# Warm-up products on one tile, another order of loads, and a written plan of the feed-forward groups in an attention and feed-forward kernel

## The chip, the core and the metric

The kernel runs on one core of a Trainium2 chip. The metric is device time in microseconds (us); the kernel before has a median of 373.9 us over 11 runs (372.59 to 376.28).

## What is computed

Sixty-four heads (8 batches of 8 heads, 576 positions, head size 64) of causal attention with a bias that falls with the running sum of relu(s), and then a feed-forward layer with a hard-swish gate over all 4608 tokens:

```python
scores = q @ k.T / 8                       # per head, 576 x 576
cum    = cumsum(maximum(s, 0))
scores = where(causal, -1e9, scores + minimum(-(cum_i - cum_j), 0))
x      = softmax(scores) @ v               # -> [4608, 512], heads side by side
h      = x @ w_in                          # [512, 2048]
g      = h * clip(h + 3, 0, 6) / 6
out    = g @ w_out                         # [2048, 512]
```

q, k, v, s, the weights and the output are float32; products take float16 operands and accumulate in float32.

## The kernel before

**Pairs and stages.** Heads are taken in 32 pairs, four to a batch (`PPB = 4`). One turn of the loop `for p in range(NP)` (L677) is a stage: scores of both heads of pair p, the exponentials, the products with v, normalisation, and the transposes that bring x into the layout of the feed-forward part. The scores of a head come in three pieces of 512 columns (`scores`, L277) and a corner for both heads (`corner`, L328). ScalarE takes the exponential (L322), VectorE applies the mask from p=5 on (L324). For p <= 4 the mask is a product instead (L285), so that the wide stair rows are not needed. `av` (L362) multiplies with v, `norm` (L390) divides by the row sum (L395, L396).

**How a pair comes in.** `load_qk` (L103) and `load_v` (L122) bring float32 into three raw buffers each (`NRAW = 3`), on the queue of SP. GpSimd casts them to float16 (`cast_qk` L173, `cast_v` L180). Pairs 0 to 3 are transposed on TensorE (L220) and copied by `order` (L199, on line L206). Pairs 4 to 8 come through a casting transfer that GpSimd issues (L110), are transposed at L228 and copied at L238. From pair 9 on the transfer engines transpose (`crossbar_qk`, L251), and `spread` copies into place. Four rows of each pair's q and k tile hold the bias; `load_aug` (L135) copies them from `rows_of`, which is worked out at the start from s (`cum1` to `cum6`, L602 to L630). Pair 0 takes its bias by products with `rows_of` and `picked` instead (L269, L314). `set_stair` (L560) fills further rows of a buffer for the pairs from 5 on.

**The front.** After the first loads are issued, `warm(22)` (L578) puts 22 idle products on TensorE (L574), each into a new tile W of one buffer with the tag "o". Then come the two transposes of pair 0 (L654, L655), `warm(4)`, and the loop.

**Feed-forward groups.** The layer works on 9 blocks of 512 tokens. `m1` (L448) is one group of four products x @ w_in (L439) into one of two "ph" banks, then ScalarE's relu with bias 3 into `tr` (L454) and VectorE's min and multiply into `gT` (L455), which frees the bank. `m2` (L459) is a group of four products gT @ w_out (L466); every fourth of a token tile is followed by a copy (L475) and a store (L477). A stage has fixed places where `group()` (L502) is called: seven at p=4 and eight from p=5 on. `group` takes m1 and m2 in turn: m1 if the last was not m1 and the block's x is there, else m2 if `m2_ready` allows it (two more m1 done than it needs, and from block 1 on 12 more m1 than m2, `LAG = 12`), else the place stays empty. Block n can begin when batch n of attention is done (block 8 with batch 7). After the last stage the rest is done without attention between.

**Queues.** Each engine works its instructions in the order in which the code issues them. SP's queue holds loads, the transposing transfers and the stores; GpSimd's holds the casts, the casting transfers (tok, w_in, w_out) and the bias rows. A transfer that waits for a buffer holds all behind it on its queue. The parts of w_in and w_out are placed by the table `weights_in` (L669) and line L664: w_in part 0 ahead of the loop, part 1 at p=2, part 2 at p=3, part 3 and the first two of w_out at p=4, and two of w_out at each of p=5, 6, 7.

Of the kernel before, what the change touches and what calls it, by code (L numbers as in the profile page):

```python
# [9 lines left out]
F32 = mybir.dt.float32  # L10
# [8 lines left out]
def kernel(  # L19
# [10 lines left out]
    nc = tc.nc  # L30
# [7 lines left out]
    NP = NHEADS // 2  # L38
    PPB = H // 2
# [4 lines left out]
    NPE = 2 * PPB + 1  # L44
# [1 line left out]
    NRAW = 3  # L46
    VW = 66
    NROW = 1
    NWARM = (22, 4)

# [49 lines left out]
    def flat(p):  # L100
        return p < PPB or p >= NPE

    def load_qk(p, i, eng=nc.sync):  # L103
        b, h0 = p // PPB, 2 * (p % PPB)
        src = (q, k)[i][b, h0 : h0 + 2]
        if not flat(p):
            if not i:
                tok = work.tile([128, 24 * D], F16, tag="tok", bufs=4, name="tok")
                toks[p] = tok[0:96].rearrange("p (i h e d) -> p i h e d", i=2, h=2, e=6)
            nc.gpsimd.dma_start(  # L110
                out=toks[p][:, i].rearrange("p h e d -> p h (e d)"),
                in_=src.rearrange("h (p e) d -> p h (e d)", e=6),
            )
# [345 lines left out]
    def m2(n, i):  # L459
        t4, fq = 2 * (i // 8) + i % 2, i % 8 // 2  # L460
        if fq == 0:
            po = psum.tile([128, 512], F32, tag="po", bufs=2, name="po")
            pos[n, t4] = po
        po = pos[n, t4]
        for ft in range(4 * fq, 4 * fq + 4):
            mm(  # L466
                po,
                lhsT=gTs[n][:, ft, t4 * 128 : (t4 + 1) * 128],
                rhs=w_out_sb[:, ft, :],
                start=(ft == 0),  # L470
                stop=(ft == NFT - 1),
            )
        if fq == 3:
            ob = work.tile([128, 512], F32, tag="ob", bufs=3, name="ob")
            nc.vector.tensor_scalar_mul(out=ob, in0=po, scalar1=1.0 / 6.0)  # L475
            r = n * 512 + t4 * 128
            nc.sync.dma_start(out=out[r : r + 128, :], in_=ob)  # L477
# [2 lines left out]
    m2_list = [(n, i) for n in range(NBLK) for i in range(16)]  # L480
    done = {1: 0, 2: 0}
    last = [2]
    tail = [False]
    LAG = 12

    def m1_ready():
        i = done[1]
        if i >= len(m1_list):
            return False
        return (512 * m1_list[i][0] + 511) // SEQ < x_done[0] // PPB  # L490

    def m2_ready():
        i = done[2]
        if i >= len(m2_list):
            return False
        n, j = m2_list[i]
        need = 16 * n + (4 * (j // 2) + 4 if j < 8 else 16)
        if done[1] == len(m1_list):
            return True
        return done[1] >= max(need + 2, i + LAG if n else 0)  # L500

    def group():  # L502
        a, c = m1_ready(), m2_ready()
        if not (a or c):
            return False
        if a and (last[0] == 2 or (tail[0] and not c)):
            m1(*m1_list[done[1]])
            done[1] += 1
            last[0] = 1
        else:  # L510
            if c:
                m2(*m2_list[done[2]])
                done[2] += 1
            last[0] = 2
        return True


    C = {}
# [8 lines left out]
    load_qk(0, 0)  # L527
    load_qk(0, 1, nc.scalar)
    nc.scalar.preload_act_table_set("natural_log_exp_and_others")
    for p in (1, 2):  # L530
        for i in range(2):
            load_qk(p, i)
        load_v(p - 1, nc.sync)
    for i in range(NROW):
        fill(nc.gpsimd, qks[i][64:68, :, :, :], 0.0)
    fill(nc.gpsimd, ident, 0.0)
# [32 lines left out]
    fill(nc.vector, xT[:, 0, 0:512], 0.0)  # L569

    def warm(n):
        for _ in range(n):
            W = psum.tile([128, 512], F32, tag="o", name="W")
            nc.tensor.matmul(  # L574
                W, lhsT=xT[:, 0, 0:128], rhs=xT[:, 0, 0:512], start=True, stop=True
            )
# [65 lines left out]
    cum1(0, V)  # L642
    cum2(0)
    cast_qk(0, nc.scalar.copy)
    for i in range(2):
        load_qk(3, i)
    load_v(2, nc.sync)
    cum3(0, V)
    nc.scalar.copy(out=rows_of[0][0:32, 0, 0:SEQ], in_=C["c"][0:32])
    cum4(0, V)  # L650
# [5 lines left out]
    warm(NWARM[1])  # L656
    for g in range(1, 2 * NROW):
        pick(g)
    load_aug(1, nc.gpsimd)
    cast_qk(1)  # L660
    load_aug(2, nc.gpsimd)
    cast_v(0)
    cast_qk(2)
    load_w_in(0)  # L664
    cast_v(1)


    I, U = load_w_in, load_w_out
    weights_in = {  # L669
        2: ((I, 1),),  # L670
        3: ((I, 2),),
        4: ((I, 3), (U, 0), (U, 1)),
        5: ((U, 2), (U, 3)),
# [2 lines left out]
    }  # L676
    for p in range(NP):  # L677
        nxt = p + 1 < NP
        if p + 3 < NP:
            load_v(p + 3, nc.sync)  # L680
        if p == 1:
            nc.sync.dma_start(out=stair_sb, in_=stair_dram.ap())
        if NPE <= p + 4 < NP:
            for i in range(2):
                load_qk(p + 4, i)
        if PPB <= p < PPB + 3:
            set_stair((p + 1) % NQK, nc.gpsimd.tensor_copy)
            load_aug(p + 1, nc.gpsimd)
        c = p + 2
        if p and c < NP and flat(c):  # L690
            cast_qk(c)
            if c >= NPE:
                crossbar_qk(c)
        if p and nxt:
            cast_v(p + 1)
        if p and p < NP - 2 and not PPB <= p + 1 < PPB + 3:
            load_aug(p + 2, nc.gpsimd)
        for fn, c in weights_in.get(p, ()):
            fn(c)
        if p and PPB <= p + 3 < NPE:  # L700
            for i in range(2):
                load_qk(p + 3, i)
        if p == 10:
            load_s(1, (nc.sync,) * 4)
            fill(nc.gpsimd, rows_of[1][:, 0, :], 1.0)
        if p == 11:
            cum1(1, nc.gpsimd)
        if p == 12:
            cum2(1)
            nc.gpsimd.tensor_copy(out=rows_of[1][0:32, 0, 0:SEQ], in_=C["c"][0:32])  # L710
        if p == 13:
            cum3(1, nc.gpsimd)
            cum4(1, nc.gpsimd)
        if p == 13:
            cum5(1, nc.gpsimd)
            cum6(1, nc.gpsimd)

        def get(i):
            if p + 1 < NPE:
                transpose(p + 1, i)  # L720
            elif nxt:
                spread(p + 1, i)

        if p < PPB:
            scores(p, 0, 0)
            scores(p, 0, 1)
# [12 lines left out]
            av(p, 0, 0)  # L739
            scores(p, 1, 2)  # L740
            av(p, 0, 1)
            norm(p, 0)
            continue

        if p == PPB:
            early[0] = False
            scores(p, 0, 0)
            av(p - 1, 1, 0)
            m1_begin(0, 0, NKC - 1)
            av(p - 1, 1, 1)  # L750
            norm(p - 1, 1)
            scores(p, 0, 1)
            m1_begin(0, 1, NKC - 1)
            transpose_x(p - 1)
            group()
            group()
            scores(p, 0, 2)
            get(0)
            nc.vector.tensor_scalar(
                out=masks, in0=shut, scalar1=65504.0, scalar2=None, op0=ALU.add  # L760
            )
        else:
# [24 lines left out]
        av(p, 0, 1)  # L787
        norm(p, 0)
        group()
# [6 lines left out]
    group()  # L796
    group()
    transpose_x(p)
    tail[0] = True
    while group():  # L800
        pass
# [28 lines left out]
```

## Time and profile before

| | |
|---|---|
| median of 11 runs | 373.9 us |
| profiled execution, own time | 375.43 us |
| its span | 373.4 us |
| TensorE products busy (PE) | 358.1 us, 96% |
| VectorE (DVE) | 244.2 us, 65% |
| ScalarE (ACT) | 219.7 us, 59% |
| GpSimd (POOL) | 130.6 us, 35% |
| m2 products L466 | 576, 146.1 us |
| m1 products L439 | 576, 149.0 us |
| idle products L574 | 26, 585 ns each |
| HBM read, written | 37.36 MB, 9.44 MB |

All times come from one profiled execution. A line of a timeline has start, duration, engine, source line, operation, what is written from what, the tile's size, how often; in square brackets the idle time just before and what ended it. PE is TensorE's products, PEld its loads of weights, SPq or POOLq the issue of a transfer. In the rows over the span each digit is a fortieth of it, in tenths.

### The profile page before, as it was taken

To read this page: it belongs to the slowest core of one execution; us is meant where nothing else is said; L and a number is where in the kernel's file an instruction comes from. 1 tells how busy PE (TensorE), PEld (TensorE's weight loads), DVE (VectorE), ACT (ScalarE), POOL (GpSimd) and SP (SyncE) were. 2 spreads that over 40 slices of the span, in tenths; PEclk is the share of its full clock that TensorE was granted. 3 is DMA by queue.
4 is the path that set the end of the run, shared out by engine and by line. 5 is a ranking of instruction groups with operands and counts; after the bars stand their busy time and mean duration, and the time that the engine had idled before them with its cause. 6 is when DMAs were issued, how large, how long until landed. Compare 5 with 4: busy or idle time off the path is not lost.

```text
span 373.4 us, 7780 instructions
## 1 busy us (share of the span) xinstructions
PE 358.1 (96%) x2892; PEld 193.3 (52%) x2892; DVE 244.2 (65%) x551; ACT 219.7 (59%) x382; POOL 130.6 (35%) x227
## 2 busy tenths in 40 slices
PE   7999888989999999999999999999999999999995
PEld 1277555555555555555555555555555544444442
DVE  7148687757689987676767676767675635445541
ACT  3158776766667666666666666666666443434420
POOL 4849896553255933333333333333100000000000
PEclk9999999989999999999999999999999999999999
DMA  9989999994889698969787999697711101101102
GB/s 184 205 164 163 207 206 217 185 197 108 177 208 169 155 202 159 206 148 197 163 185 170 204 149 208 143 190 164 125 62 37 56 0 58 56 0 59 56 36 77
DMA packets 158262, 52.76 MB, mean 141 GB/s; under 512 B 146969, under 2 KB 153113, under 8 KB 158225
## 3 DMA queue, kind: packets, MB, share of 16 engines
q1 hardware_dynamic: 148608, 45.58, 58.9%
q0 software_dynamic: 8352, 6.25, 10.6%
q10 hardware_dynamic: 1264, 0.44, 0.6%
q8 instruction: 22, 0.36, 0.4%
q14 instruction: 16, 0.12, 0.1%
HBM read 37.36 MB, written 9.44 MB: 125 GB/s over the span
## 4 chain that ended last, share of the span: by engine, by line
PE 88%; DVE 8%; ACT 2%; issue 1%
PE po L466 32%; PE ph L439 31%; PE O L373 7%; PE S L303 7%; PE W L574 4%; PE S L292 3%; DVE gT L455 2%; DVE qk L238 2%; ACT tr L454 1%; PE pt L220 1%; DVE x L396 1%; PE ptx L410 1%; DVE qk L206 1%; DVE P L324 1%; PE S L285 1%
## 5 line engine op out<-in xcount | busy, mean ns | idle before, releaser
L455 DVE SCALAR_TENSOR_TENSOR gT<-tr,ph 128x512 f16<-128x512 f32 x144 | 98.5, 684 | 86.8 <-ACT tr L454 85.7
L439 PE MATMUL ph<-xT,w_in_sb 128*128 128x512 f16 x576 | 149.0, 380 | 1.5 <-DVE gT L455 0.9
L466 PE MATMUL po<-w_out_sb,gT 128*128 128x512 f16 x576 | 146.1, 379 | 1.2 <-DVE x L396 1.2
L454 ACT ACTIVATE tr<-ph,bias 128x512 f32<-128x512 f32 x144 | 99.0, 687 | 80.4 <-PE ph L439 71.0
L322 ACT ACTIVATE P<-S 128x512 f16<-128x512 f32 x192 | 111.8, 594 | 45.7 <-PE S L292 24.5
L439 PEld LDWEIGHTS <-w_in_sb 128*128 128x128 f16 x576 | 51.8, 98 | 45.2 <-issue 1.7
L466 PEld LDWEIGHTS <-gT 128*128 128x128 f16 x576 | 49.8, 97 | 46.8 <-DVE x L396 1.4
L138 POOL DMA_DIRECT2D qk<-rows_of x62 | 36.0, 582 | 73.5 <-PE S L303 62.4
L303 PE MATMUL S<-qk 68*128 68x448 f16 (+3 forms) x256 | 49.8, 276 | 0.8 <-ACT P L322 0.8
L373 PE MATMUL O<-va,P 128*128 128x65 f16 x896 | 48.2, 193 | 0.8 <-DVE x L396 0.8
L373 PEld LDWEIGHTS <-P 128*128 128x128 f16 x896 | 39.8, 97 | 15.0 <-DVE x L396 1.3
L182 POOL CAST va<-vraw 128x512 f16<-128x512 f32 x32 | 19.8, 617 | 53.3 <-issue 29.9
L303 PEld LDWEIGHTS <-qk 68*128 68x128 f16 x256 | 24.0, 99 | 25.7 <-issue 1.7
L206 DVE COPY qk<-jt 64x768 f16<-64x768 f16 x92 | 33.5, 365 | 3.5 <-DMA jt<-tok 2.1
L178 POOL CAST tok<-raw 128x576 f16<-128x576 f32 x52 | 34.2, 686 | 1.9 <-DMA raw<-in_k_dram 1.3
L396 DVE TENSOR_TENSOR x<-O,rl 128x320 f16<-128x320 f32 x64 | 31.5, 492 | 2.2
L475 DVE TENSOR_SCALAR ob<-po 128x512 f32<-128x512 f32 x36 | 24.6, 683 | 7.0 <-PE po L466 7.0
L324 DVE TENSOR_TENSOR P<-P,masks_sb 128x512 f16<-128x512 f16 x54 | 24.6, 456 | 4.3 <-ACT P L322 4.3
L292 PEld LDWEIGHTS <-qk 128*128 128x128 f16 (+1 forms) x256 | 19.7, 99 | 14.9 <-issue 2.4
L292 PE MATMUL S<-qk 128*128 128x128 f16 (+1 forms) x256 | 25.3, 221 | 0.7 <-ACT P L322 0.6
L574 PE MATMUL W<-xT 128*128 128x512 f16 x26 | 15.2, 585 | 2.6 <-DVE xT L164 1.2
L206 DVE COPY qk<-pt 64x768 f16<-64x768 f16 (+1 forms) x14 | 6.8, 487 | 12.9 <-PE pt L220 12.7
(69 smaller groups left out, 175.2 us busy)
## 6 DMA issues: line engine op xcount, KB each, us to landing
out_dram<-ob SPq DMA_DIRECT2D x36, 256.0 KB, 2.1
vraw<-in_v_dram SPq DMA_DIRECT2D x64, 128.0 KB, 2.8
raw<-in_q_dram SPq DMA_DIRECT2D x27, 288.0 KB, 3.8
raw<-in_k_dram SPq DMA_DIRECT2D x26, 288.0 KB, 4.3
w_in_sb<-in_moe_w_in_dram POOLq DMA_DIRECT2D x4, 512.0 KB, 7.6
w_out_sb<-in_moe_w_out_dram POOLq DMA_DIRECT2D x8, 256.0 KB, 7.1
vraw<-in_v_dram SPq DMA_DIRECT2D x32, 32.0 KB, 2.9
qk<-rows_of POOLq DMA_DIRECT2D x62, 9.0 KB, 3.1
```

Of the source, the lines that this page charges most:

```text
L138: eng.dma_start(out=qks[p % NQK][64:68, hh, :, 64 * hh : 64 * hh + SEQ], in_=rows_of[g // 32].rearrange("(r g) i t -> g r i t", g=32)[g % ...
L178: copy(out=toks[p][:, c], in_=raws[p % NRAW][:, c])
L206: copies[par](out=qk[0:64, :, i, 128 * par : 128 * par + 256 * n].rearrange("p h (s two c) -> p h s two c", two=2, c=128)[:, :, :, 0, :], ...
L292: mm(S[:, c], lhsT=kT[rows, c], rhs=qT[rows, c], start=(j == 0 and not by_product), stop=(j == 3),)
L303: mm(S[:, c : c + w], lhsT=kT[0:68, 128 * j : 128 * (j + 1)], rhs=qT[0:68, 128 * (j + 1) : SEQ], start=(c == 0), stop=(c != 0 and p >= NROW),)
L322: nc.scalar.activation(out=pt[:, c], in_=S, func=AF.Exp, scale=0.125)
L373: mm(o[:, i, :], lhsT=lhsT, rhs=va[:, hh, j, 0:65], **kw)
L396: nc.vector.tensor_tensor(out=X[p][:, :, hh, :], in0=o[:, :, 0:64], in1=rl.to_broadcast([128, 5, 64]), op=ALU.mult,)
L439: mm(ph, lhsT=w_in_sb[:, kc, ft * 128 : (ft + 1) * 128], rhs=xT[:, kc, n * 512 : (n + 1) * 512], start=(kc == 0), stop=(kc == NKC - 1),)
L454: nc.scalar.activation(out=tr, in_=ph, func=AF.Relu, bias=bias3[:, 0:1])
L455: nc.vector.scalar_tensor_tensor(out=gTs[n][:, ft, :], in0=tr, scalar=6.0, in1=ph, op0=ALU.min, op1=ALU.mult)
L466: mm(po, lhsT=gTs[n][:, ft, t4 * 128 : (t4 + 1) * 128], rhs=w_out_sb[:, ft, :], start=(ft == 0), stop=(ft == NFT - 1),)
```

## The change

1. `warm` makes its tile W once and not for each product; the first call makes 16 products and not 22.
2. The bias rows of pairs 1 to 4 are issued on SP and not on GpSimd. SP's loads for pairs 1 to 3 are placed around them: bias rows of 1, q and k of 2, bias rows of 2, v of 1, q and k of 3, v of 2. Pair 4's casting transfers move ahead of the loop.
3. w_in parts 0 and 1 are issued in stage p=2 on GpSimd, behind the casts of the first batch; before, part 0 was issued ahead of the loop.
4. Inside a stage, casts and weights now come ahead of `load_v`, of the casting transfers of p+3 and of `set_stair` with its bias rows. The raw q and k of a pair from 9 on are loaded three stages ahead and not four.
5. `group` follows a written plan in stages 4 to 7 (1 is m1, 2 is m2, a dot is an empty place). After it, m1 may follow m1 where no m2 is ready, `LAG` is 7 for all blocks, and where nothing else can be done m2 may use an m1 that was done just before.

```diff
-    NWARM = (22, 4)
+    NWARM = (16, 4)
...
-    tail = [False]
-    LAG = 12
+    LAG = 7
+    plan = list("1111.11" + "11.11.1." + "12.12.12" + "12122222")
...
-    def m2_ready():
+    def m2_ready(slack):
...
-        return done[1] >= max(need + 2, i + LAG if n else 0)
+        return done[1] >= need + slack and (not slack or done[1] >= i + LAG)
...
     def group():
-        a, c = m1_ready(), m2_ready()
-        if not (a or c):
-            return False
-        if a and (last[0] == 2 or (tail[0] and not c)):
+        if plan:
+            what = plan.pop(0)
+            a, c = what == "1", what == "2"
...
+        else:
+            a, c = m1_ready(), m2_ready(2)
+            if not a and not c:
+                c = m2_ready(0)
+        if a and (last[0] == 2 or not c):
             m1(*m1_list[done[1]])
...
     def warm(n):
+        W = psum.tile([128, 512], F32, tag="o", name="W")
         for _ in range(n):
-            W = psum.tile([128, 512], F32, tag="o", name="W")
...
-    load_aug(1, nc.gpsimd)
+    load_aug(1, nc.sync)
+    for i in range(2):
+        load_qk(2, i)
+    load_aug(2, nc.sync)
+    load_v(1, nc.sync)
+    for i in range(2):
+        load_qk(3, i)
+    load_v(2, nc.sync)
     cast_qk(1)
-    load_aug(2, nc.gpsimd)
     cast_v(0)
     cast_qk(2)
-    load_w_in(0)
-    cast_v(1)
+    for i in range(2):
+        load_qk(4, i)
...
     for p in range(NP):
         nxt = p + 1 < NP
+        if 0 < p < PPB - 1:
+            load_aug(p + 2, nc.sync)
+        if NPE <= p + 3 < NP:
+            for i in range(2):
+                load_qk(p + 3, i)
+        c = p + 2
+        if p == 1:
+            cast_v(1)
+            cast_qk(3)
+        elif p == 2:
+            load_w_in(0)
+            cast_v(2)
+            cast_v(3)
+            load_w_in(1)
+        elif p:
+            if NPE <= c < NP:
+                cast_qk(c)
+                crossbar_qk(c)
+            if nxt:
+                cast_v(p + 1)
+            for fn, c in weights_in.get(p, ()):
+                fn(c)
         if p + 3 < NP:
             load_v(p + 3, nc.sync)
...
+        if 2 <= p and PPB < p + 3 < NPE:
             for i in range(2):
-                load_qk(p + 4, i)
+                load_qk(p + 3, i)
         if PPB <= p < PPB + 3:
             set_stair((p + 1) % NQK, nc.gpsimd.tensor_copy)
             load_aug(p + 1, nc.gpsimd)
...
+        if p > PPB + 1 and p < NP - 2:
             load_aug(p + 2, nc.gpsimd)
```

Nothing in what is computed changes.

More of the change, by code (lines that the diff above doesn't have):

```diff
@@ L499, in m2_ready @@
             return True
-        return done[1] >= max(need + 2, i + LAG if n else 0)
+        return done[1] >= need + slack and (not slack or done[1] >= i + LAG)
     def group():
-        a, c = m1_ready(), m2_ready()
-        if not (a or c):
-            return False
-        if a and (last[0] == 2 or (tail[0] and not c)):
+        if plan:
+            what = plan.pop(0)
+            a, c = what == "1", what == "2"
+            assert not a or m1_ready()
+            assert not c or m2_ready(0)
+        else:
[3 more added lines that the diff above has]
+        if a and (last[0] == 2 or not c):
             m1(*m1_list[done[1]])
@@ L509, in group @@
             last[0] = 1
[L510 to L513, printed above, removed]
+        elif c:
+            m2(*m2_list[done[2]])
+            done[2] += 1
             last[0] = 2
-        return True
+        return a or c
     C = {}
@@ L529 @@
     nc.scalar.preload_act_table_set("natural_log_exp_and_others")
[L530 to L533, printed above, removed]
+    for i in range(2):
+        load_qk(1, i)
+    load_v(0, nc.sync)
     for i in range(NROW):
@@ L644 @@
     cast_qk(0, nc.scalar.copy)
-    for i in range(2):
-        load_qk(3, i)
-    load_v(2, nc.sync)
     cum3(0, V)
@@ L658 @@
         pick(g)
-    load_aug(1, nc.gpsimd)
+    load_aug(1, nc.sync)
[6 more added lines that the diff above has]
+    load_v(2, nc.sync)
     cast_qk(1)
-    load_aug(2, nc.gpsimd)
     cast_v(0)
     cast_qk(2)
-    load_w_in(0)
-    cast_v(1)
+    for i in range(2):
+        load_qk(4, i)
     I, U = load_w_in, load_w_out
     weights_in = {
-        2: ((I, 1),),
         3: ((I, 2),),
@@ L678 @@
         nxt = p + 1 < NP
+        if 0 < p < PPB - 1:
+            load_aug(p + 2, nc.sync)
+        if NPE <= p + 3 < NP:
+            for i in range(2):
+                load_qk(p + 3, i)
[16 more added lines that the diff above has]
+                fn(c)
         if p + 3 < NP:
             load_v(p + 3, nc.sync)
-        if p == 1:
+        if p == 2:
             nc.sync.dma_start(out=stair_sb, in_=stair_dram.ap())
-        if NPE <= p + 4 < NP:
+        if 2 <= p and PPB < p + 3 < NPE:
             for i in range(2):
-                load_qk(p + 4, i)
+                load_qk(p + 3, i)
         if PPB <= p < PPB + 3:
@@ L688 @@
             load_aug(p + 1, nc.gpsimd)
[L689 to L696, printed above, removed]
-            load_aug(p + 2, nc.gpsimd)
[L698 to L702, printed above, removed]
+        if p > PPB + 1 and p < NP - 2:
+            load_aug(p + 2, nc.gpsimd)
         if p == 10:
@@ L798 @@
     transpose_x(p)
-    tail[0] = True
     while group():
```

## The prediction

> **What bounds the kernel now.** I read the slices of the span first, then the timeline of the first 40 us, then the busy time by stage, then the loop from a first product (m1, L439) to its gate (L455).
>
> ```profile
> PE   7999888989999999999999999999999999999995
> ...
> PEclk9999999989999999999999999999999999999999
> ...
> DMA  9989999994889698969787999697711101101102
> ```
>
> TensorE (PE) is busy from end to end, so the time is PE's own work plus the stretches where it works for nothing or waits. The transfers are near full for the first 80 us, one slice being 9.3 us. The timeline says what the first slices are:
>
> ```profile
> 1.20 14.05 PE L574 MATMUL W<-xT 128*128 128x512 f16 x22 [1.20 <-DVE xT L164]
> ...
> 1.86 0.10 PEld L574 LDWEIGHTS <-xT 128*128 128x128 f16 x1 [0.54 <-issue]
> ...
> 6.04 1.25 ACT L178 CAST tok<-raw 128x576 f16<-128x576 f32 x2 [2.61 <-DMA raw<-in_q_dram]
> ...
> 8.68 0.37 DVE L633 TENSOR_SCALAR picked<-rows_of,sel 128x576 f16<-128x576 f16 x1
> ...
> 15.96 1.01 DVE L206 COPY qk<-pt 64x768 f16<-64x768 f16 x2 [6.91 <-PE pt L220]
> ...
> 18.96 0.63 PE L285 MATMUL S<-shut,ident 128*128 128x512 f16 x1
> ...
> 23.26 0.39 PE L285 MATMUL S<-shut,ident 128*128 128x512 f16 x1
> ```
>
> The inputs of pair 0 are cast at 7.3 us and VectorE is ready at 9.05, but it waits 6.9 us for a transpose, since PE is still in its 22 idle products, one each 0.64 us. The same 512-column product takes 0.63 us at 18.96 and 0.39 at 23.26: the first stage runs on a half-rate array although the row of granted clocks shows none of it. Later stages, busy time by stage (width, then PE, PE loads, VectorE, ScalarE, GpSimd; clock, DMA share, GB/s):
>
> ```profile
> 38.05:47.40 9.35, 7.69 (x88) 4.61 (x85) 6.41 (x12) 6.72 (x13) 8.09 (x13) 1.00 1.24 207
> ...
> 57.16:67.24 10.08, 8.61 (x90) 5.25 (x89) 7.43 (x16) 6.48 (x12) 6.56 (x12) 1.00 1.21 222
> ...
> 76.63:83.50 6.87, 5.48 (x58) 3.64 (x57) 4.12 (x12) 4.24 (x9) 3.43 (x7) 0.78 1.00 205
> ...
> 196.00:205.20 9.20, 9.20 (x82) 5.14 (x81) 7.11 (x18) 6.25 (x12) 3.24 (x7) 1.00 0.80 171
> ```
>
> In stages p=4 to 8 PE idles 1 to 2 us a stage and at p=8 loses its clock (0.78); from 130 us, in p=14, to 250 it is busy 120.00 us of 120. There the order of groups can only lose.
>
> **What the Trainium skill says.** "TensorE: Matmul & The Clock Gate", section "Wait — 56ns, not 53.3ns?": products start 426.7 ns apart on a cold array and 215.7 ns apart on a warm one at 512 columns. The trace agrees on the warm figure: four m1 products take 0.86 us. The 0.64 us of the idle products is longer than the cold figure, and the 0.54 us ahead of each load shows that the difference is a wait. The same page, "What's actually happening": the clock is released after about 3.4 us of sustained work. The trace: dense work begins at 18.6 and is fast from 22.8, 4.2 us later, while 14 us of products with gaps released nothing. "DMA: Bandwidth & Descriptors", "Issuing engines are not separate DMA queues": transfers from SP, ACT and POOL share the same 16 engines. The trace shows a w_in part that takes 5.4 us to land from 30 us, in a quieter time, and 9.2 us from 33. So a part of w_in issued later leaves room for the q, k and v loads of the first batch.
>
> **The change part by part.** Sums are of the profiled execution: span 373.4, own time 375.4, so 2.0 lie around it; it is 1.5 above the median of 373.9.
>
> *Front.* One W tile removes the wait between products. 16 of them take 16 x 0.427 = 6.8 us cold (end at 8.0) or, warm after 3.4 us, 8 x 0.427 + 8 x 0.216 = 5.1 (end at 6.3); 16 x 0.64 = 10.2 if the wait stays. Either way VectorE's 9.05 becomes the last to come. Its copy of pair 0 takes 1.01, ScalarE's, 1.40, begins after the second transposes, near 8.9; scores start at about 10.4 instead of 18.6: -8.2. Stage p=0 takes 6.68 us now (18.6 to 25.28), 1.4 of it for the half-rate array (3.81 us between 18.96 and 22.77, of which the array part halves); I take the array as warm: p=1 at 15.7. Then 4.09, 4.09 and 4.59 as now (25.28, 29.37, 33.46, 38.05): p=4 at 28.5, which is -9.5.
>
> *Loads.* Both bias-row loads (aug) go to SP, and SP waits in its queue for the rows, finished at 8.65. Behind it stand q and k of pair 2, v of 1, q and k of 3, v of 2. SP is free at 7.95 now, so this queue loses 0.7 us and four issues of 0.6, 3.1 us in all. q and k of 2 issued at 9.9 to 11.1 land 4.1 to 5.4 us later (as now) by 15 to 16.5, and the cast is 1.3; they are needed near 16.5. v of 1 and pair 3 come out within 1 us of need too. GpSimd loses eight aug issues of 0.59 (4.7 us), which is what lets the casts run ahead. I cost this at 0, bounds -0.3 (less queueing behind w_in) and +4 (if each stage waits 1 us for a load). w_in 0 is issued at about 21.3 and lands 5.4 to 9.2 later, 27 to 30.5, for a need at 29: inside the same bounds.
>
> *The step to p=5.* The stair copy and aug of pair 5 went behind cast_v, three weight issues and two q/k issues on GpSimd: 0.9 + 0.8 + 1.45 + 1.3 = 4.5 us. Now the copy begins at 35.17 (2.45), the two aug issues at 37.55 (1.18) land 6.5 to 6.9 us later, by 45; the product that needs them is at 47.4: about 2.5 us of cover. After: the items up to pair 6's loads end at about 29.8 on GpSimd (the chain cast of pair 3, w_in 0, casts of v 2 and 3, w_in 1, loads of 5, cast of v 4, w_in 2, loads of 6, each by its time now and the landing of its v), +4.5 +2.45 +1.2 = 38.0, landed 4 (as the aug issued at 9.3) to 6.9 us after the issue, at 41 to 44. p=4 would end at 38.8. I take +3.0, ends 0 and +5.
>
> *Plan, p=4 to 8.* Groups (0.863 us each) by stage are 4, 6, 6, 6, 1 now and 6, 5, 6, 8, 8 after. What remains of a stage now when its groups are taken off: 5.9, 4.6, 4.9, 4.2, and for p=8 about 5.2 (its one group half-rate). More groups fill some of the idle time: I take 5.1, 4.7, 4.5, 3.9, 3.3. Sum after: 33 x 0.863 + 21.5 = 50.0, plus the 3.0 is 53.0 against 45.45 now, for 10 groups more. p=9 starts at 81.5 (now 83.5).
>
> *Groups later.* p=9 to 11 as now, 9.22 each, p=12 with 7 groups 8.4, p=13 with 4 groups 6.8. By the end of attention 212 groups are done after, 201 now: 11 x 0.863 = 9.5 us leave the tail.
>
> *Runs of m1.* This is the price. With LAG 7 and "m1 again where no m2 is ready" the backlog of m2 is drained at each batch's end, so each batch starts with seven m1 in a row (second half of p=13, 17, 21, 25, 29 and after), and a triple two stages later; p=8 and 9 have a run of five. Now m1 and m2 alternate. There are two ph banks, so an m1 waits for the gate two before it:
>
> ```profile
> 46.52 1.02 PE L439 MATMUL ph<-xT,w_in_sb 128*128 128x512 f16 x4 [0.67 <-DVE gT L455]
> ...
> 196.19 1.03 PE L439 MATMUL ph<-xT,w_in_sb 128*128 128x512 f16 x4
> ...
> 197.25 0.69 ACT L454 ACTIVATE tr<-ph,bias 128x512 f32<-128x512 f32 x1 [0.27 <-PE ph L439]
> ...
> 198.05 0.67 DVE L455 SCALAR_TENSOR_TENSOR gT<-tr,ph 128x512 f16<-128x512 f32 x1
> ```
>
> Start to freed bank is 2.5 us unloaded; two slots of PE are 2.0 to 2.6 (0.86 each, with 0.22 to 0.47 of attention between). Written out for a run of seven with exp 0.60, tr 0.69, gate 0.69, mask 0.43, spread 0.67 and norm 0.69 in program order, the third, fifth and seventh m1 wait 0.4, 0.4 and 0.5: 8.28 us become 9.6. So 1.3, and 0.15 for the triple: 1.45 a batch, five times 7.3, and 0.8 for the run of five: +8.1. Bounds: +3 (0.5 a batch, if exps come early) and +15 (2.7, if each m1 in a run waits 0.4).
>
> *Sum.* 81.5 + 27.7 + 0.8 + 8.4 + 6.8 = 125.2 at p=14 (now 126.1); 18 stages of 9.21 and 7.3: 298.3 (now 291.9); the rest is 81.5 now, less 9.5: 72.0. That is 370.3, -3.1: own time 372.3, and median 370.8.
>
> **Rivals.** (1) The above, 370.8; its own range 367 to 375. (2) The runs cost 0.5 a batch and the stair copy is in time: -3.1 - 3.0 - 5.1 = -11.2, 362.7. For it: from p=14 VectorE is busy 7.1 of 9.2 and ScalarE 6.3, and runs are followed by m2 that let them catch up. Against: two more m1 bring VectorE to 8.5, and the wait of 0.67 at 46.52 is there with single m1. (3) Slower: one mechanism, the runs of m1 on two ph banks in p=13 to 31. All else is worth -11.2; 5.6 batches break even at 2.0 a batch. At 3.2 it is 380.6. For it: in-order ScalarE puts an exp of 0.60 ahead of each tr, and a late m1 delays the next scores, so waits feed each other. Against: my row of seven gives 1.3. (4) The loads, not PE, set the first batch: the change does not do what it says, p=4 starts near 32 and 3.5 come back: 374.3. For it: DMA share 1.22 with 209 GB/s in the first 15 us. Against: 129 GB/s between 22.8 and 30, so there is room to load earlier.
>
> **How the numbers follow.** (1) 0.42, (2) 0.27, (3) 0.17, (4) 0.14. About 0.3% (1.1 us) is what can be told from no change, 372.8 to 375.0. Faster: 0.34 from (1), all of (2) and 0.04 from (4): 0.65. Same: 0.06 from (1), 0.07 from (4) and 0.02 from (3): 0.15. Slower: 0.20. The range: 361 leaves out a third of (2), 378 about half of (3).
>
> **What would show it.** Right: 16 products 0.43 us or less apart, first scores near 10.4 at 0.39 a product, p=4 near 28.5, about 81.5 at p=9, a wait on the p=5 rows near 39, waits of PE's m1 on the gate of 0.3 to 0.5 three times in each batch, 72 us after the last attention stage. Wrong: idle products still 0.64 apart; scores waiting for q, k or v in p=1 to 3; stage p=18 not longer than 9.2 (case 2) or over 11.5 (case 3); a slice of low clock near 39.

## The result, and the profile after

The kernel after has a median of 388.3 us over 12 runs (385.9 to 390.4); the kernel before has 374.4 over the runs beside it. The ratio is 1.0371, 95% interval 1.035 to 1.0392: slower by 13.9 us, where 3.1 faster was forecast and 378 was the upper end of the range. The profiled execution has a span of 387.3 and an own time of 389.1.

Starts of some stages in the profiled executions, in us (forecast, where the prediction or its sums give one):

| | p=0 | p=4 | p=5 | p=9 | p=13 | p=14 | p=31 | end |
|---|---|---|---|---|---|---|---|---|
| before | 18.96 | 38.05 | 47.40 | 83.50 | 119.36 | 126.12 | 283.54 | 373.4 |
| forecast | 10.4 | 28.5 | 41.8 | 81.5 | 118.4 | 125.2 | | 370.3 |
| after | 9.08 | 31.15 | 50.68 | 91.50 | 129.18 | 139.96 | 305.74 | 387.3 |
| after less before | -9.9 | -6.9 | +3.3 | +8.0 | +9.8 | +13.8 | +22.2 | +13.9 |

A lead of ten microseconds at the first stage is a lag of eight by p=9. Three stretches do it: p=1 to 3 (three of the ten), p=4 (another ten) and p=5 to 8 (five); then p=13 costs four, the stages from 14 to 31 eight, and the tail gives eight back.

The slices of the span, from the page of the kernel after:

```profile
PE   8978378999998789998999999989999999999995
...
PEclk9999779999999989999999999999999999999998
DMA  9799997567798997789898977898943001101102
```

The 3 and the 7 behind it in the row of PE, with a clock of 0.7 below both, are new: slices 5 and 6, from 38.7 to 58 us. Slice 14, from 126 us, has another 7, and the clock is 0.8 in the slice behind it. Next, the front, from the timeline of the kernel after (start, duration, engine, line, operation, and in brackets the idle time ahead and what ended it):

```profile
1.20 6.14 PE L578 MATMUL W<-xT 128*128 128x512 f16 x16 [1.20 <-DVE xT L164]
...
6.40 1.25 ACT L178 CAST tok<-raw 128x576 f16<-128x576 f32 x2 [2.97 <-DMA raw<-in_q_dram]
...
9.08 0.38 PE L285 MATMUL S<-shut,ident 128*128 128x512 f16 x1
```

Sixteen idle products take 6.14 us, 0.38 each instead of 0.64, and the first score product takes 0.38 where it took 0.63: the array is warm. The front does what the prediction said of it. Busy time by stage (width, then PE, PE loads, VectorE, ScalarE, GpSimd; clock, DMA share, GB/s), for p=4, 13, 18 and 19 of the kernel after:

```profile
31.15:50.68 19.53, 9.54 (x93) 5.44 (x93) 8.42 (x16) 8.54 (x16) 14.14 (x22) 0.83 1.25 210
129.18:139.96 10.78, 7.61 (x70) 4.25 (x67) 8.59 (x16) 5.48 (x10) 7.69 (x11) 0.84 1.15 191
178.80:189.35 10.55, 9.53 (x81) 5.26 (x80) 7.88 (x18) 7.43 (x13) 3.61 (x6) 1.00 0.85 152
189.35:198.67 9.32, 9.32 (x81) 5.22 (x80) 7.96 (x19) 6.65 (x12) 3.40 (x6) 1.00 0.77 156
```

Stage p=4 is 19.53 us wide and PE works 9.54 of them. Stage 13 has 3.2 idle, 18 has 1.0, 19 none. PE's waits in the kernel after (total, times, longest) name the causes:

```profile
PE S L292 <- DMA qk<-rows_of: 8.5, 1, 8.5
PE ph L439 <- DVE gT L455: 7.1, 9, 2.5
PE po L466 <- DVE gT L455: 3.5, 6, 1.0
PE Sc L344 <- DMA qk<-rows_of: 2.1, 1, 2.1
```

Before, the gate (L455) cost m1 0.9 us in two waits and m2 nothing, and the bias rows never appeared among the waits. The row of 8.5 is one wait, of pair 5, and GpSimd's timeline shows how its rows came to be late:

```profile
28.99 0.61 POOL L182 CAST va<-vraw 128x512 f16<-128x512 f32 x1 [2.13 <-DMA vraw<-in_v_dram]
...
34.96 0.61 POOL L182 CAST va<-vraw 128x512 f16<-128x512 f32 x1 [2.51 <-DMA vraw<-in_v_dram]
...
36.50 1.43 POOL L154 DMA_DIRECT2D w_out_sb<-in_moe_w_out_dram  x2
37.91 0.67 POOL L110 DMA_DIRECT2D tok<-in_q_dram  x1
...
39.25 2.45 POOL L566 COPY qk<-stair_sb 64x1280 f16<-64x1280 f16 x2
41.64 1.20 POOL L138 DMA_DIRECT2D qk<-rows_of  x2
```

Two casts stand 2.1 and 2.5 us waiting for v, and with them all that is behind them on GpSimd. Then come one part of w_in, two of w_out and two casting loads, and only then the stair copy and the two bias rows of pair 5. The rows land 8.5 to 8.9 us after their issue; they took 6.5 to 6.9 before. On PE:

```profile
50.68 0.58 PE L292 MATMUL S<-qk 128*128 128x128 f16 x4 [8.50 <-DMA qk<-rows_of]
...
51.54 1.91 PE L439 MATMUL ph<-xT,w_in_sb 128*128 128x512 f16 x4
```

Four m1 products take 1.91 us after the wait and 1.02 before it: the idle stretch cost the clock too. "TensorE: Matmul & The Clock Gate", section "What's actually happening", in the Trainium skill, says that the array falls back to half rate after about 3.4 us of idleness and needs as much work to recover. At 8.5 us of idleness the trace agrees. But less was enough elsewhere in this case: in p=13 of the same kernel a wait of 2.54 is followed by four products in 1.86, while in the kernel of the first experiment one of 2.10 is followed by 1.02. Which idleness it takes was not measured.

### The profile page after: what moved, and what is told of

Read it like the earlier page. It is cut to its first block, busy times and chain, and to the rows that moved or that the text cites. A ratio compares the mean times of both kernels' runs of the same rounds, so it can differ in the third digit from the quotient of the medians.

```text
span 387.3 us, 7712 instructions
## 1 busy us (share of the span) xinstructions
PE 354.2 (91%) x2886; PEld 193.2 (50%) x2886; DVE 251.3 (65%) x551; ACT 218.7 (56%) x382; POOL 128.4 (33%) x219
## 4 chain that ended last, share of the span: by engine, by line
PE 71%; DVE 11%; DMA 7%; ACT 5%; issue 2%; SPq 2%; POOL 1%
PE po L466 31%; PE ph L439 27%; PE O L373 5%; PE S L303 5%; DVE gT L455 4%; DMA qk<-rows_of 4%; ACT tr L454 3%; PE S L292 3%; DVE qk L206 2%; DMA raw<-in_q_dram 2%; DMA raw<-in_k_dram 2%; DVE P L324 1%; ACT P L322 1%; DVE x L396 1%; ACT qk L238 1%
## 5 line engine op out<-in xcount | busy, mean ns | idle before, releaser
L455 DVE SCALAR_TENSOR_TENSOR gT<-tr,ph 128x512 f16<-128x512 f32 x144 | 98.1, 684 | 74.7 <-ACT tr L454 73.9
L466 PEld LDWEIGHTS <-gT 128*128 128x128 f16 x576 | 50.6, 97 | 51.6 <-DVE gT L455 6.5
L178 POOL CAST tok<-raw 128x576 f16<-128x576 f32 x52 | 35.5, 686 | 61.4 <-DMA raw<-in_q_dram 45.5
L138 POOL DMA_DIRECT2D qk<-rows_of x54 | 31.7, 587 | 63.5 <-PE S L303 54.9
L324 DVE TENSOR_TENSOR P<-P,masks_sb 128x512 f16<-128x512 f16 x54 | 26.2, 484 | 17.9 <-ACT P L322 17.9
L206 DVE COPY qk<-jt 64x768 f16<-64x768 f16 x92 | 36.6, 398 | 1.1
L182 POOL CAST va<-vraw 128x512 f16<-128x512 f32 x32 | 20.2, 632 | 25.8 <-PE O L373 14.9
L395 DVE RECIPROCAL rl<-O 128x5 f32<-128x5 f32 x64 | 12.1, 189 | 17.0 <-PE O L373 17.0
L352 ACT ACTIVATE PC<-Sc 128x128 f16<-128x128 f32 x32 | 8.8, 276 | 8.7 <-PE Sc L344 8.7
```

The source lines that it names most:

```text
L138: eng.dma_start(out=qks[p % NQK][64:68, hh, :, 64 * hh : 64 * hh + SEQ], in_=rows_of[g // 32].rearrange("(r g) i t -> g r i t", g=32)[g % ...
L178: copy(out=toks[p][:, c], in_=raws[p % NRAW][:, c])
L206: copies[par](out=qk[0:64, :, i, 128 * par : 128 * par + 256 * n].rearrange("p h (s two c) -> p h s two c", two=2, c=128)[:, :, :, 0, :], ...
L455: nc.vector.scalar_tensor_tensor(out=gTs[n][:, ft, :], in0=tr, scalar=6.0, in1=ph, op0=ALU.min, op1=ALU.mult)
L466: mm(po, lhsT=gTs[n][:, ft, t4 * 128 : (t4 + 1) * 128], rhs=w_out_sb[:, ft, :], start=(ft == 0), stop=(ft == NFT - 1),)
```

## The experiments

In the expectations, A is the account formed from the two traces: the warm front gains, and the late stair step, the runs of m1 with what happens in p=13, and waits for loads lose more. The other letters name what each expectation itself puts against it. Each interval is of the ratio to the kernel before on the same chip.

### The stair step, first in its stage

The edit moves the block of the stair copy and its bias rows from the end of GpSimd's work in p=4 to 6 to its beginning, as it stood before; all else is the kernel after:

```diff
         nxt = p + 1 < NP
+        if PPB <= p < PPB + 3:
+            set_stair((p + 1) % NQK, nc.gpsimd.tensor_copy)
+            load_aug(p + 1, nc.gpsimd)
         if 0 < p < PPB - 1:
...
-        if PPB <= p < PPB + 3:
-            set_stair((p + 1) % NQK, nc.gpsimd.tensor_copy)
-            load_aug(p + 1, nc.gpsimd)
```

> The changed kernel with the stair copy and its bias rows at the head of stages 4 to 6 again, ahead of the casts, the weight issues and the casting transfers. Theory A (their place behind these on GpSimd made the wait of 8.5 us ahead of p=5): p=5 starts near 42 us instead of 50.7, the clock isn't lost there, about 378 us. Theory B (the transfers are full, so the rows land late wherever they are issued): p=5 still after 48, 386 to 389 us.

Measured: 379.7 us, ratio 1.0136 (1.0091 to 1.0181), against 1.0371 for the kernel after: by the ratios 8.8 us come back from a move of three lines. p=5 starts at 42.85 instead of 50.68, and p=4 is 13.4 wide. From the timeline of this kernel:

```profile
36.27 2.54 POOL L566 COPY qk<-stair_sb 64x1280 f16<-64x1280 f16 x2 [3.08 <-DMA stair_sb<-stair]
38.76 1.20 POOL L138 DMA_DIRECT2D qk<-rows_of  x2
```

The copy itself now waits 3.1 us, because the changed kernel loads `stair_sb` one stage later (at p=2), so there was more to gain. The two rows of pair 5 land 3.5 to 4.0 us after issue here; the last weights and casting loads ahead of them on GpSimd were issued six us before. A held for p=5, but the clock is lost after all, one stage later:

```profile
53.60 0.38 PE L292 MATMUL S<-qk 128*128 128x128 f16 x4 [2.55 <-DMA qk<-rows_of]
```

The rows of pair 6 are waited for, and the granted clock is 0.5 from 54.4 to 57.6 us.

### The same step, with w_out out of its way

Only the first two parts of w_out move from p=4 to p=5; the stair block stays last:

```diff
-        4: ((I, 3), (U, 0), (U, 1)),
-        5: ((U, 2), (U, 3)),
+        4: ((I, 3),),
+        5: ((U, 0), (U, 1), (U, 2), (U, 3)),
```

> The changed kernel with the first two parts of w_out issued in stage 5 and not 4, behind the stair copy of pair 5 and not ahead of it. Theory A (what is issued ahead on GpSimd's queue holds the copy and the landing of the rows): the rows are issued 1.4 us earlier and land 6 to 7 us after it and not 8.7, p=5 starts near 47, 383.5 to 385.5 us. Theory B (the transfers are full, order doesn't count): 387 to 389 us.

Measured: 385.6, ratio 1.0343 (1.0285 to 1.0401). One of PE's waits in this kernel:

```profile
PE S L292 <- DMA qk<-rows_of: 5.4, 2, 4.5
```

The long wait is 4.5 instead of 8.5. The copy begins at 37.38 (39.25 in the kernel after) and the rows land 6.3 to 6.6 after issue instead of 8.5 to 8.9, so both terms are smaller: 1.9 us by the earlier issue and about 2 by the shorter landing. That the landing is shorter because the parts of w_out are out of its way is not shown: with the old groups, below, the rows land 5.9 to 6.1 us after issue behind the same three weight parts as in the kernel after. The medians differ by 2.7, and the intervals overlap, so it is the stage that shows the gain and not the total.

### The idle products alone

The kernel before with one W tile and sixteen products:

```diff
-    NWARM = (22, 4)
+    NWARM = (16, 4)
...
     def warm(n):
+        W = psum.tile([128, 512], F32, tag="o", name="W")
         for _ in range(n):
-            W = psum.tile([128, 512], F32, tag="o", name="W")
```

> The kernel before with the single W tile and 16 idle products, nothing else. Theory A (the front was held by the idle products alone): first scores at 9 to 10 us, p=4 at 29 to 31, some of it given back at p=5 since GpSimd's chain moves less; 366 to 369 us. Theory C (the old order of loads can't follow an earlier front): p=1 to 4 wait for casts and rows, 372 to 375 us.

Measured: 372.1, ratio 0.9948 (0.9921 to 0.9976): 1.9 us, less than A set; it is C's number. The lead over the kernel before is 10.0 us at p=0, 9.5 at p=3, 4.3 at p=4, 1.4 at p=6 and 2.8 at p=9, and stays there. PE's timeline in this kernel says where it goes:

```profile
23.33 0.41 PE L373 MATMUL O<-va,P 128*128 128x65 f16 x8 [0.67 <-POOL va L182]
...
26.05 0.38 PE L292 MATMUL S<-qk 68*128 68x128 f16 x4 [1.67 <-DMA qk<-rows_of]
...
28.57 0.66 PE L228 MATMUL pt<-ident,tok 96*128 96x96 f16 x6 [1.92 <-DMA tok<-in_q_dram]
```

Three waits for loads in p=2 and 3, 4.3 us, none of which the kernel before has: for v of pair 2, the bias rows of pair 3, and q of pair 4. They also leave PE at half rate (granted clock 0.5 from 26.6 to 33.3): the first score product of the next head takes 0.63, at 30.98, where it took 0.38 at 24.01. The other 2.8 go in p=5, with waits of 1.6 and of 0.6 for w_out and again a clock of 0.5, from 50.5 to 53.8; 1.4 come back in p=8, where the kernel before is at 0.5 and this one is not. A front that is ten microseconds quicker meets inputs that are not.

### Are the weights what delays those inputs?

Two kernels leave out the loading of three quarters of w_in and w_out and use the first quarter in the place of the others, so that their output is not the layer's. The edit is the same on the kernel before and on that with the idle products alone:

```diff
-                lhsT=w_in_sb[:, kc, ft * 128 : (ft + 1) * 128],
+                lhsT=w_in_sb[:, kc, ft % 4 * 128 : (ft % 4 + 1) * 128],
...
-                rhs=w_out_sb[:, ft, :],
+                rhs=w_out_sb[:, ft % 4, :],
...
-    weights_in = {
...
+    weights_in = {4: ((U, 0), (U, 1))}
```

> The kernel before with only a quarter of each weight loaded (part 0 of w_in, the first two of w_out) and used in place of the rest, so that the output is not the layer's; all products stay. It is the base of the next run. Both theories: the old front leaves room for the loads, 372 to 374.5 us.

> The same with the single W tile and 16 idle products; three quarters of the weights are left out in the same way. Theory G (the lead of 10 us at p=0 is lost because the transfers carry the first batch and the weights no faster): p=4 near 29, lead over few_weights_before 7 to 9 us at the end. Theory H (it is lost on the engines, as in waits on VectorE and GpSimd's own work): p=4 near 33, lead 2 to 3 us as with all weights.

Measured: on the kernel before 374.7, ratio 0.9995 (0.9979 to 1.0012), so no cost of the weights is seen in that kernel. With the warm front 369.9, ratio 0.9869 (0.984 to 0.9897): by the ratios the front is worth 4.7 us here and 1.9 with all the weights, each within about 1 us. So the weights take some 2.8 us of the lead, and in the profiles they take it in p=4 and 5: p=6 starts at 53.4 here and at 55.8 with all of them. But the rest is not back: p=4 still starts at 33.96, and PE still waits ahead of it, with three quarters of the weights gone:

```profile
28.48 0.66 PE L228 MATMUL pt<-ident,tok 96*128 96x96 f16 x6 [2.07 <-DMA tok<-in_q_dram]
```

The waits for v of pair 2 and for the bias rows of pair 3 are there too (0.7 and 1.4 us), so these loads are late without the weights. Neither of the two expectations holds alone.

A third kernel moves only part 0 of w_in behind p=1, where the changed kernel has it:

```diff
-    load_w_in(0)
...
-        2: ((I, 1),),
+        2: ((I, 0), (I, 1)),
```

> warm_only with part 0 of w_in issued in stage 2 and not ahead of the loop: the one part of the weights that stands among the loads of pairs 2 to 4 in the queue. Theory G: v of pair 2 lands 1.5 to 2.5 us earlier, p=4 near 32, 370 to 371.5 us. Theory H: 372 to 373 us.

Measured: 371.7, ratio 0.9936 (0.9909 to 0.9962). p=4 starts at 32.0 instead of 33.75, in one profile each (a kernel below that is the same up to p=11 starts it at 30.2). It is the lowest time of all kernels here with the whole layer, but it can't be told from the idle products alone.

### The groups alone, and all but the groups

First the kernel before with the new `plan`, `LAG` and `group`, and then the kernel after with the old ones; the edit is that part of the diff:

```diff
-    tail = [False]
-    LAG = 12
+    LAG = 7
+    plan = list("1111.11" + "11.11.1." + "12.12.12" + "12122222")
...
+            if not a and not c:
+                c = m2_ready(0)
+        if a and (last[0] == 2 or not c):
```

> The kernel before with the plan, the rule without strict turns and LAG 7, nothing else. Theory A (runs of m1 cost more than the places filled are worth): p=4 to 8 5 us longer for 10 groups more, p=13 4 us longer, p=14 to 31 8 us longer, 9.5 us less in the tail: 380 to 385 us. Theory D (all of the loss of the changed kernel is the wait at p=5, the groups are worth what they fill): 366 to 371 us.

> The changed kernel with the old plan of groups (strict turns, LAG 12), so the front and the order of loads alone. Theory A: p=4 at 31, p=5 still near 50 for want of the bias rows, then as the kernel before with a lead of -3 (a lag of 3): 376 to 379 us. Theory D: 382 to 388 us, since the wait at p=5 is all there is.

Measured: the groups alone 385.6, ratio 1.0289 (1.0246 to 1.0332). Its p=14 and p=31 start 163.1 apart against 157.4 before, and its p=13 is 11.35 wide against 6.8. In its profile 1.9 us of the loss stand already at p=1, before any group, and are not of the groups. All but the groups: 379.9, ratio 1.0132 (1.0077 to 1.0188), with the late stair step again (p=5 at 51.4, after a wait of 11.4). GpSimd's timeline in this kernel has a longer wait for v ahead of the same items:

```profile
38.05 0.66 POOL L182 CAST va<-vraw 128x512 f16<-128x512 f32 x1 [6.08 <-DMA vraw<-in_v_dram]
```

So the groups alone make a slower kernel, and the rest of the change alone does too.

### The loads with the old groups and the stair step first

The same as the last, with the stair block moved as in the first experiment.

> The changed kernel with the stair copy first in stages 4 to 6 and the old plan of groups: the front and the loads as a whole without the two parts that cost. Theory A (the two costs are the stair copy's place and the runs of m1, and they add up): p=5 near 43 us, then as the kernel before with a lead of 4.5, some of it lost to weights; 369 to 372 us. Theory B (the transfers set the time to p=9 whatever the order): 374 to 377 us.

Measured: 374.1, ratio 0.9994 (0.9973 to 1.0015). This is B's number and not A's: the new order of loads, with its worst place mended, gives away the 1.9 us of the idle products (the two intervals just touch). B's reason, full transfer engines whatever the order, is not shown by it. p=5 starts at 44.1, after a wait of 2.5 for its rows; the stair copy waited 2.0 for `stair_sb`; q or k of a pair waits 2.7 for its cast, and two parts of w_out are waited for, 1.7 in all.

With these five kernels the loss can be walked in steps, each a difference of two measured ratios times 374.4: idle products -1.9; loads, with the stair step first, +1.7; groups +5.3; stair step last +8.8; sum +13.9. Each interval is 1 to 2 us to either side, so the two small steps are the least sure. The steps depend on the order: the groups cost 10.8 on the kernel before and 5.3 on this one, and the stair step 5.2 with the old groups and 8.8 with the new.

### Not letting the m2 drain

On the kernel of the first experiment, m2 may do without its lag only while sixteen m1 or fewer are done, which is what the plan's end needs. The backlog of m2 is then kept, so no batch starts with a row of m1 and no m2 follows at once on the m1 that it needs; in p=11 to 13 fifteen places stay empty (the expectation says 23), ten more than with the drain:

```diff
-            if not a and not c:
+            if not a and not c and done[1] <= 16:
                 c = m2_ready(0)
```

> stair_first, but from block 1 on no m2 is taken before its lag of 7, so that a backlog of m2 stays and m1 and m2 alternate from p=13 on; 23 places in p=11 to 13 stay empty for it. Theory A (the runs of m1 cost 5 to 6 us in p=14 to 31 and 2 to 4 in p=13): stages from p=14 at 9.26 us again, p=11 and 12 shorter by 5, tail longer by 8.6: 373 to 376 us. Theory F (the stages got longer for another reason, as the closer loads): stages from p=14 stay at 9.6, 380 to 383 us.

Measured: 373.6, ratio 0.9998 (0.9976 to 1.002), against 1.0136 with the drain. The spans are 370.5 and 378.9. Of these 8.4, 7.3 are there by p=14 (125.1 against 132.4): 1.0 by p=9, where the two kernels are still the same, and 6.1 in p=11 and 12, which have ten groups less. Another 8.1 follow by p=31, and 7.0 are given back in the tail, which has those ten groups. One late stage of this kernel, by the same columns as above:

```profile
166.67:175.89 9.22, 9.22 (x82) 5.15 (x80) 6.43 (x17) 6.17 (x11) 4.19 (x8) 1.00 1.01 205
```

9.22 with PE busy throughout, against 10.55 for p=18 of the kernel after. A held for the stages from p=14: the drain is what makes them long. For p=13 it did not: that stage is 8.91 wide here and 9.03 with the drain. The edit takes away two things at once, the runs of m1 and the m2 right behind its m1. What a row of m1 looks like, in p=18 of the kernel after:

```profile
180.35 1.72 POOL L178 CAST tok<-raw 128x576 f16<-128x576 f32 x2 [2.80 <-DMA raw<-in_q_dram]
...
180.66 1.55 DVE L206 COPY qk<-jt 64x768 f16<-64x768 f16 x2
...
182.24 1.28 DVE L455 SCALAR_TENSOR_TENSOR gT<-tr,ph 128x512 f16<-128x512 f32 x2
182.99 1.02 PE L439 MATMUL ph<-xT,w_in_sb 128*128 128x512 f16 x4 [1.02 <-DVE gT L455]
```

Two copies of the pair to come (L206) run 1.55 us on VectorE, where the pair takes 0.66 elsewhere; two gates stand behind them, and the m1 waits 1.02 for the first of the two: both ph banks are full. The copies run beside GpSimd's casts, and both are longer than alone (two casts take 1.28 to 1.32 in the late stages of the kernel before, clear of the copies). The casts wait for raw q, which this kernel loads three stages ahead and not four. With the groups alone, and four stages, they do not wait: the copies of p=18 take 0.65, no m1 waits there, and the stage is 9.65 wide. So the runs of m1 are hit a second time where a late stage puts a copy beside a cast; the next section shows that more plainly.

The m2 that follows at once costs too, in p=16 of the kernel after:

```profile
160.97 1.02 PE L439 MATMUL ph<-xT,w_in_sb 128*128 128x512 f16 x4
...
162.26 0.81 PE L466 MATMUL po<-w_out_sb,gT 128*128 128x512 f16 x3
163.49 0.39 PE L466 MATMUL po<-w_out_sb,gT 128*128 128x512 f16 x1 [0.42 <-DVE gT L455]
```

Its fourth product needs the gate of the m1 just ahead. The same wait of 0.42 stands in p=20, 24 and 28, and each of these four stages is 9.81 wide and not 9.22.

### The stage p=13

In p=13 of the kernel after, GpSimd works out bias rows of the second half in float32 (L625 to L634) while a row of m1 is going. From its timeline:

```profile
130.28 1.28 POOL L625 TENSOR_TENSOR r<-c,rows_of 64x576 f32<-64x576 f32 x1
130.40 1.43 DVE L324 TENSOR_TENSOR P<-P,masks_sb 128x512 f16<-128x512 f16 x1
...
131.76 2.10 DVE L206 COPY qk<-jt 64x768 f16<-64x768 f16 x2
132.44 1.27 POOL L634 TENSOR_TENSOR rows_of<-r,rows_of 32x576 f16<-32x576 f32 x1
...
136.71 1.86 PE L439 MATMUL ph<-xT,w_in_sb 128*128 128x512 f16 x4 [2.54 <-DVE gT L455]
```

The mask takes 1.43 instead of 0.42, and the pair of copies 2.10 instead of 0.66. "SBUF — State Buffer", section "Who interferes with whom", in the Trainium skill, says that VectorE and GpSimd share a pair of ports, that an operation with two inputs in SBUF, or a copy in a two-port mode, is held up whole by a GpSimd operation that reads there, and that who issues first goes first. The trace agrees: the mask began 0.12 after L625 and ended 0.27 after it; the copies, begun beside L630, ended 0.15 after L634. On the kernel of the first experiment, the edit moves these steps to p=12:

```diff
-        if p == 13:
             cum3(1, nc.gpsimd)
             cum4(1, nc.gpsimd)
-        if p == 13:
             cum5(1, nc.gpsimd)
```

> stair_first with GpSimd's last four steps on the bias rows of batches 4 to 7 moved from stage 13 to stage 12, where all groups are m2. Theory E (GpSimd's arithmetic stretches VectorE's copies, and at p=13 that falls on a run of m1): stage p=13 from 9.0 to about 7 us, p=12 up to 1 us longer, 377 to 378.5 us. Theory A alone (the run of m1 would stall p=13 anyway): 379.5 to 380.5 us.

Measured: 379.0, ratio 1.0142 (1.0089 to 1.0196), no difference from 1.0136. But stage 13 is 7.13 wide instead of 9.03, and stage 12 is the same (8.36 and 8.37). In stage 13 of this kernel:

```profile
125.60 0.43 DVE L324 TENSOR_TENSOR P<-P,masks_sb 128x512 f16<-128x512 f16 x1
126.04 0.66 DVE L206 COPY qk<-jt 64x768 f16<-64x768 f16 x2
```

The 1.9 us are shown in the stage, of which p=14 gives 0.6 back (10.4 wide and not 9.8); the time of the kernel does not tell it, with intervals 4 us wide. The steps alone do not cost this: with the old groups and the steps in p=13 the stage is 6.8 wide. It takes the row of m1 and the steps together.

The same edit on the kernel with idle products and w_in part 0 late, which has no rows of m1:

> The same, and GpSimd's four steps on the later bias rows in stage 12 and not 13. Theory E (they stretch VectorE's copies in stage 13): stage 13 from 6.8 to 6 us, 0.5 us less than warm_w_in_late. Otherwise the same time.

Measured: 374.1, ratio 0.9993 (0.9974 to 1.0013), 2.5 us more than without the edit. In the two profiles 2.8 us are there at p=9 (82.6 against 79.9), before anything the edit touches; p=12 to 14 then take 25.8 against 24.2, so the edit costs 1.6 here, where VectorE's copies of the next pair stand beside the steps in p=12. Stage 13 is 7.35 wide and not 6, so E did not hold on this kernel.

## Why the prediction was wrong, by its own steps

*Front.* Right, and a little more came: scores at 9.08 instead of 10.4, sixteen products in 6.14 us between the two values given, the array warm at the first score.

*Loads, at 0 with bounds -0.3 and +4.* The number was inside the bounds but the value taken was not right: p=4 at 31.15 instead of 28.5, +2.65. The bias rows of pair 3, issued at 21.74 on SP, are waited for 2.1 us. This is rival (4), and it is not a matter of the changed order alone: even without the new order the front's lead of ten falls to four by p=4. I took that VectorE's 9.05 was the last to come, but behind it stood the inputs of p=3 and 4, which the slow front had covered in the kernel before. The 129 GB/s between 22.8 and 30, which the prediction counted as room, was no proof that they could come earlier. All seven kernels with this order start p=4 later than 28.5 (29.4 to 33.0).

*The step to p=5, at +3.0 with ends 0 and +5.* This is the step that failed most: p=4 took 19.53 us instead of 13.3, and with the late start p=5 came 8.9 later than forecast. By its terms: GpSimd ended the loads of pair 6 at 32.45, not 29.8, a cast having waited 2.1 for v (+2.65); the next cast waited 2.5 for v, which the sum did not have (+2.5); the four items of 4.5 took 4.3; the copy and two issues were right (2.45 and 1.2), so the issue ended at 42.8 instead of 38.0. The landing was 8.7 where 4 to 6.9 was taken. The sum counted what each item costs GpSimd and forgot what each item may wait for. The first experiment shows that the place of the block is the cause; the second makes the landing 2 us shorter, for a reason that is not shown. The prediction's own sign of being wrong, a slice of low clock near 39, is what the profile shows.

*Plan, p=4 to 8.* 81.5 was forecast for p=9 and 91.50 came; 8.9 of the 10.0 were there at p=5. From p=5 to p=9 it took 40.8, where 39.7 was forecast: right within 1.1, though the half-rate array after the long wait is in it.

*Groups later.* p=9 to 12 took 37.7 against 36.9; one wait of 1.0 in p=11 is an m2 behind the m1 that it needs. p=13 took 10.78 and not 6.8: +4.0, where the prediction had no run of m1 under GpSimd's float32 steps. Moving the steps takes 1.9 off this stage on the kernel of the first experiment, where it is 9.03 wide. The other 1.75 can be read from the two traces: the wait at the gate is 2.54 and not 2.10, and 1.3 come behind it, where the next two m1 take 1.86 and 1.35 at half rate and not 1.02 and 1.03.

*Runs of m1, at 1.45 a batch.* Right as a mechanism; that the sum came near (from p=14 to p=31 it took 165.8 instead of 157.4, +8.4, where +7.3 was set for eighteen stages) is in part luck. The runs by themselves cost less: with the groups alone, whose copies stand clear of the casts, the three stages of a batch that have runs are 0.4, 0.1 and 0.4 longer, 0.9 in all, where 1.45 was set. Two things that the prediction did not have make up the rest. An m2 that waits for the m1 just ahead of it makes p=16, 20, 24 and 28 each 0.6 longer, 2.4 in all. And in p=14, 18, 22 and 26 an m1 waits once, 0.6 to 1.0, behind copies that take 1.1 to 1.55 beside casts where the working had 0.67 for a spread; the whole stretch took 5.7 more with the groups alone and 8.4 here. Of PE's 7.1 us at the gate 3.2 lie in these four waits, not three of 0.4 to a batch. Rival (3), 3.2 a batch, was not needed for a slower kernel.

*Tail, at -9.5.* From p=31 to the end 81.56 against 89.9 before, -8.3. Right within 1.2.

Forecast to measured, the sum is 2.65 + 6.2 + 1.1 + 0.8 + 4.0 + 2.2 (p=14 to the end) = 17.0 = 387.3 - 370.3. What was not seen is that the groups do not pay for themselves: where the drain is taken away, 14.4 us are saved from p=9 to 31 (6.3 by p=14, 8.1 after it) and only 7.0 lost in the tail, and the sum in the prediction had -9.5 against +8.1 and so left them about even. The ten groups in p=11 and 12 cost there nearly what they save in the tail (6.1 against 7.0), so the long stages from p=14 are almost pure loss.

Open: what the runs of m1 cost without the m2 that follows at once, since no run has one without the other; which order of the first batch's loads would keep the front's lead, and how much of each load's lateness is the full transfer engines and how much its place in the queue. The share was 1.0 and 182 GB/s from p=0 to p=4 in the kernel after, but no run took the two apart. Kernels with the same order up to p=4 reach it between 29.4 us (stair step first) and 33.0 (without the drain), in one profile each, which puts a limit on what a single one says of such waits; why they differ was not found.

## What to carry to other kernels

A step that is moved back on an in-order queue costs the durations of the items that it is moved behind and also every wait those items may have (2.1 and 2.5 us here, 6.1 with the old groups): ask for each item what it waits for, before its time is added. When a stall at the front is taken away, go through the inputs of the next stages one after another with their landing times, since the stall may have been their cover. A rule that empties a backlog turns an even alternation into runs, runs fill the two banks between the engines, and a consumer taken right behind its producer waits out the whole chain between them: price both ahead of the work that they bring forward.

## What the runs showed of the hardware

A bias row of 9 KB that GpSimd issues landed 3.5 to 4.0 us after issue where the last weights and casting loads of that engine were issued six us before (stair step first). Where they were issued about three us before it took longer, but not by their number: 6.3 to 6.6 behind one weight part and two casting loads (w_out later), 8.5 to 8.9 behind three and two (the kernel after), 5.9 to 6.1 behind the same three and two (old groups). "DMA: Bandwidth & Descriptors", section "Issuing engines are not separate DMA queues", says that transfers from all engines end up on the same sixteen and interleave; so what else was under way may set the landing as much as what the same engine issued before, and no run here takes the two apart. An idle stretch of 2.54 us in a stage with other gaps was followed by products at half rate, one of 2.10 was not. GpSimd's float32 steps stretched a VectorE mask from 0.42 to 1.43 us and a pair of copies from 0.66 to 2.10, and its casts a pair of copies to 1.55.
